# K transposed by VectorE in 32x32 word blocks, scores with a block-diagonal q

## The chip, the cores and the metric

The kernel runs on one core of one Trainium2 chip. The time is device time in microseconds (us) of one execution; the number that counts is the median of several executions without a profile. The engines of a core work side by side and meet at semaphores: TensorE (PE) multiplies matrices, with the loading of its weights shown as a row of its own (PEld); VectorE (DVE) and ScalarE (ACT) work on elements; GpSimd (POOL) only clears buffers here; SyncE (SP) issues the loads. Sixteen DMA engines move data between HBM and the on-chip memory SBUF. PE writes its results into PSUM, a second on-chip memory of eight banks.

## The reference

It is one decode step: attention of one token over a long cache, mixed with a small MLP by a gate. In bfloat16, cut to what matters:

```
x: 1 x 448;  k_cache, v_cache: 8 heads x 65536 rows x 256;  wq: 448 x 4096;  wo: 4096 x 448
q = (x @ wq)                         # 16 query heads of 256, two for each head of K and V
scores = q . k * 256 ** -0.5         # 16 x 65536
o = softmax(scores) @ v              # 16 x 256
a = o @ wo                           # 1 x 448
b = the MLP of layernorm(x)          # 1 x 448, 1792 hidden units, weights of length 1792
g = sigmoid(sum(x * gate_w))
out = g * a + (1 - g) * b
```

K and V are 268 MB each, so 537 MB are read to make 448 numbers.

## The kernel before, in words

**Blocks.** The cache is worked on in 32 blocks (`NBLK`), four for each K/V head. A block has 16384 rows of one head; each of the 128 SBUF partitions gets 128 consecutive rows. So a block has 8.4 MB of K, loaded as two halves into the tiles `kn0` and `kn1` (`load_k`, L109), and 8.4 MB of V, loaded into the one tile `vt` (`load_v`, L115). The loads are issued on SP's queue in a fixed order: V of block n, then both halves of K of block n+1, then V of block n+1. Each waits until its tile has been read: a half of K for the transposes of the block before, V for the products of the block before. `wo` (3.7 MB) follows after the K of block 1. In the last block V goes into the freed `kn` tiles in eight pieces that get smaller (`load_v_last`, L124). V of the block before the last comes in two parts, 48 rows for each partition before the last K and 80 behind it.

**Scores (`score_block`, L349).** To multiply q with K, the 256 elements of a row must lie across partitions. The kernel reads two bfloat16 neighbours as one 32-bit word and has PE transpose 128x128 words at a time (L326); four of them fill a PSUM bank `tps`, and DVE copies the bank into `kT` (L331). There are two `kT` tiles and four `tps` banks. A `kT` tile holds 16 rows of each partition (index i, 0 to 7), so a block has 8 such steps and 32 quarters. With `kT` in place, `scores` (L340) multiplies: for each of the two elements of a word (c), four matmuls of 32 columns of `qpad` against 512 columns, each in its own quarter of the PE array. All 8 steps add into one bank `sc_ps`: partition 32a + 2i + r holds the scores of step i, quarter a and query head r. `qpad` has zeros everywhere but in the two columns of its step.

**Softmax and products.** `softmax` (L400) takes the maximum over the bank, exchanges it between partitions by small matmuls, lets ACT take the exponential into `p_sb`, and has DVE transpose that into `pT` in 32x32 blocks (L432). `products` multiplies `pT` with V: 64 matmuls (L368), four of which run side by side. `accumulate` (L442, L447) adds the result, rescaled, to `acc`.

**End.** In the last block the pieces of V go through `columns` (L393), where the block of V is the weight, as they land. Then one DVE instruction makes `oT` (L579), four matmuls with `wo` (L584) add into one PSUM row `f_ps` that already holds the rest of the result, DVE copies its first half (L588), ACT its second (L589), and the row is stored (L590).

**Order.** The helper `seq` ties every instruction to the one before it on its engine, so each engine works in the order in which the program names its instructions. Between the quarters of a block small pieces of other work are hooked in: `gate_sum` and `mixer_tail` in block 0, `gate_column` in block 1, and in the last block `result_base` and a part of the products of the block before.

Of the kernel before, what the change touches and what calls it, by code (L numbers as in the profile page):

```python
# [8 lines left out]
FP32 = mybir.dt.float32  # L9
BF16 = mybir.dt.bfloat16  # L10
# [4 lines left out]
HQ = 16  # L15
HKV = 8
DH = 256
REP = HQ // HKV
# [3 lines left out]
KP = VP // 2  # L22
NJ = 16
NI = VP // NJ


@with_exitstack
def kernel(
# [15 lines left out]
    nc = tc.nc  # L44

    D = A_x.shape[-1]
# [4 lines left out]
    NB = SK // BLK  # L51
    NBLK = HKV * NB
# [36 lines left out]
    hd_ps = psum.tile([128, 512], FP32, name="hd_ps")  # L89

# [84 lines left out]
    qpad = const.tile([128, 2, HKV, NI, 32], BF16)  # L175
    seq(nc.gpsimd.memset(qpad[:], 0.0))


    xm = const.tile([128, 3], BF16)
# [62 lines left out]
    for h in range(HQ):  # L242
        half, hh = divmod(h, HQ // 2)
        for c in range(2):
# [13 lines left out]
                start=False,  # L258
                stop=True,
            ))  # L260
    seq(nc.vector.tensor_copy(
        out=qpad[:, :, :, 0, 0:REP],
        in_=q_ps.rearrange("p (c g r) -> p c g r", c=2, r=REP),
    ))
# [52 lines left out]
    base = const.tile([1, D], FP32)  # L317
    res = const.tile([1, D], BF16)
    gcol = const.tile([128, 1], FP32)
    state = {"t": 0}  # L320

    def transposes(i, quarter):
        tp = tps[state["t"] % 4]
        state["t"] += 1
        for jj in range(4):
            seq(nc.tensor.transpose(  # L326
                tp[:, jj * 128:(jj + 1) * 128],
                k_tiles[i // 4][:, i % 4 * NJ + quarter * 4 + jj, :].bitcast(FP32),
                ident_f[:, :],
            ))  # L330
        seq(nc.vector.tensor_copy(  # L331
            out=kT_tiles[i % 2][:, quarter * 4:(quarter + 1) * 4, :, :].rearrange(
                "p j n c -> p (j n c)"
            ),
            in_=tp[:, :].bitcast(BF16),
        ))

    def scores(g, i, c):
        for a in range(4):
            seq(nc.tensor.matmul(  # L340
                sc_ps[32 * a:32 * (a + 1), :],
                lhsT=qpad[:, c, g, i, :],
                rhs=kT_tiles[i % 2][:, :, 32 * a:32 * (a + 1), c],
                start=(i == 0 and c == 0),
                stop=(i == NI - 1 and c == 1),
                tile_position=(0, 32 * a),
            ))

    def score_block(n, hooks={}):  # L349
        due = []  # L350
        for t, (i, quarter) in enumerate((i, q) for i in range(NI) for q in range(4)):
            transposes(i, quarter)
            if due and due[0][0] <= t:
                scores(n // NB, *due.pop(0)[1])
            if quarter == 3:
                due.append((t + 2, (i, 0)))
                due.append((t + 3, (i, 1)))
            if t in hooks:
                hooks[t]()
        while due:  # L360
            scores(n // NB, *due.pop(0)[1])

    def pv(n, ip, jjs=range(NJ), tile=None, dst=pv_ps, last_ip=NI // 2 - 1):
        pT = pT_tiles[n % 2]
# [35 lines left out]
    def softmax(n, fill=None):  # L400
        b = n % NB
        fill = fill or [lambda: None] * 3
        nb, nb_old = nb_tiles[n % 2], nb_tiles[(n + 1) % 2]
        al, pT = al_tiles[n % 2], pT_tiles[n % 2]
        seq(nc.vector.tensor_reduce(out=rmax[:], in_=sc_ps[:, :], op=ALU.max, axis=AXIS.X))  # L405
        fill[0]()
        seq(nc.tensor.transpose(sm_ps[0:1, 0:128], rmax[:, 0:1], ident_f[:, :]))  # L407
        fill[1]()
        seq(nc.vector.tensor_reduce(  # L409
            out=(mrun if b == 0 else mnew)[:],  # L410
            in_=sm_ps[0:1, 0:128].rearrange("o (a i r) -> o r a i", a=4, r=REP)[:, :, :, 0:NI],
            op=ALU.max, axis=AXIS.XY,
        ))
# [10 lines left out]
        seq(nc.scalar.activation(  # L424
            out=p_sb[:, :], in_=sc_ps[:, :], func=ACT.Exp, scale=scale,
            bias=nb[:, 0:1], accum_out=den[:, 0:1],
        ))
# [4 lines left out]
        seq(nc.vector.transpose(out=pT[:, :], in_=p_sb[:, :]))  # L432
        if b > 0:
            seq(nc.vector.scalar_tensor_tensor(  # L434
                out=lsum[:], in0=lsum[:], scalar=al[:, 0:1], in1=den[:], op0=ALU.mult, op1=ALU.add
            ))
        else:
            seq(nc.vector.tensor_copy(out=lsum[:], in_=den[:]))
# [68 lines left out]
            op0=ALU.mult, op1=ALU.add,  # L507
        ))

    pv_last = sc_ps[:].rearrange("p (e d) -> p e d", e=2)  # L510
    o_last = hd_ps[:, 464:464 + 2 * REP].rearrange("p (c r) -> p c r", c=2)

    for n in range(NBLK):
        if n == 0:
            score_block(n, {8: gate_sum, 20: mixer_tail})
        elif n < L:
            score_block(n, {5: gate_column} if n == 1 else {})
        else:
            score_block(n, {4: result_base, 8: lambda: pv(L - 1, 0), 14: lambda: pv_one(L - 1, 2)})
        if n < L - 1:  # L520
            load_v(n)
            load_k(n + 1, 0)
            load_k(n + 1, 1)
            if n == 0:
                seq(nc.sync.dma_start(
                    out=wo_sb[:], in_=A_wo.rearrange("(h p c) n -> p h c n", p=128, c=2)
                ))
        elif n == L - 1:
            load_v(n, 0, 48)
            load_k(L, 0)  # L530
            load_k(L, 1)
            load_v(n, 48, VP)
        else:
            load_v_last(L)
        if n < L:
            softmax(n)
        else:
            def rest_base():
                seq(nc.tensor.matmul(
                    f_ps, lhsT=ident_f[0:1, 0:1], rhs=base[0:1, :], start=True, stop=False  # L540
                ))
                pv(L - 1, 2, range(4, NJ))

            f_ps = tps[0][0:1, 0:D]
# [36 lines left out]
    ))  # L581
    for c in range(2):
        for r in range(REP):
            seq(nc.tensor.matmul(  # L584
                f_ps, lhsT=oT[:, c, r:r + 1], rhs=wo_sb[:, HQ - REP + r, c, :],
                start=False, stop=(r == REP - 1 and c == 1),
            ))
    seq(nc.vector.tensor_copy(out=res[:, 0:D // 2], in_=f_ps[:, 0:D // 2]))  # L588
    seq(nc.scalar.copy(out=res[:, D // 2:], in_=f_ps[:, D // 2:]))  # L589
    seq(nc.sync.dma_start(out=out[0, 0].rearrange("(o n) -> o n", o=1), in_=res[:]))  # L590


# [28 lines left out]
```

## Time and profile before

| | us |
|---|---|
| median of 3 executions (1280.61 to 1280.92) | 1280.71 |
| the profiled execution | 1283.39 |
| its span, first to last instruction | 1281.6 |
| PE busy, 8663 matmuls | 986.4 |
| PE weight loads, 8663 | 642.5 |
| DVE busy, 1359 instructions | 755.2 |
| ACT busy | 43.1 |

The mean granted clock of PE is 0.853 of its full speed. The DMA engines moved 545.5 MB, 426 GB/s over the span. Busy time of PE is that of pipelined matmuls, so it overlaps itself. In rows of a group, "x1024 | 647.9, 684" means 1024 instructions, 647.9 us busy, 684 ns for one. In a timeline a row begins with its start and its length in us.

The trace also keeps one record for each packet that a DMA engine moved: its queue, its start, its bytes and how long it took. A half of K is 128 packets of 32 KB, eight for each DMA engine; a block of V is 128 packets of 64 KB, again eight for each.

### The profile page before, as it was taken

Reading aid. Unit: us, or ns where it says so; the run is one execution under the profiler, and the core shown is the slowest. Engines: PE = TensorE matmul, PEld = TensorE weight load, DVE = VectorE, ACT = ScalarE, POOL = GpSimd, SP = SyncE. Lnnn points to the kernel's source line nnn. Section 1 sums busy time; section 2 is a strip of 40 time slices with the busy share of each in tenths; the row PEclk is TensorE's granted clock in tenths of the full one; section 3 lists DMA queues with packets and bytes.
Section 4 is the critical chain, followed back from the end, with each engine's and each line's share of the span. In section 5 each row is a group of like instructions: output and inputs, shape, how many; then the busy total and the mean of one; then the engine's idle time right before and its main releaser. Section 6 shows DMA issues by size and latency. Waiting matters only on the chain.

```text
span 1281.6 us, 19942 instructions
## 1 busy us (share of the span) xinstructions
PE 986.4 (77%) x8663; PEld 642.5 (50%) x8663; DVE 755.2 (59%) x1359; ACT 43.1 (3%) x108; POOL 4.2 (0%) x7
## 2 busy tenths in 40 slices
PE   5777777797778777777876687866779777888796
PEld 4455444554545555445544455544456444555464
DVE  5464556665556655566654566644676545675483
ACT  4000000000000000000000000000000000000000
POOL 1000000000000000000000000000000000000000
PEclk9887878887888978789888889887898878898797
DMA  9999999999999999999999999999999999999896
GB/s 408 425 435 430 434 423 433 432 435 432 443 418 435 436 440 427 429 428 438 435 430 434 432 427 431 441 436 426 426 435 434 440 420 433 427 422 438 379 408 292
DMA packets 18000, 545.51 MB, mean 426 GB/s; under 512 B 2165, under 2 KB 4216, under 8 KB 4728
## 3 DMA queue, kind: packets, MB, share of 16 engines
q1 hardware_dynamic: 17474, 544.22, 98.7%
q8 instruction: 68, 1.11, 0.3%
q14 instruction: 20, 0.16, 0.0%
q10 hardware_dynamic: 438, 0.01, 0.0%
HBM read 544.22 MB, written 0.00 MB: 425 GB/s over the span
## 4 chain that ended last, share of the span: by engine, by line
DMA 69%; PE 29%; DVE 1%; issue 0%; SPq 0%; ACT 0%
DMA kn<-in_A_k_cache_dram 66%; PE tps L326 24%; PE sc_ps L340 5%; DMA vt<-in_A_v_cache_dram 2%; DMA kn<-in_A_v_cache_dram 2%; DVE kT L331 1%; PE tps L584 0%; DMA xr<-in_A_x_dram 0%; DVE z L279 0%; DVE zt L278 0%; DVE res L588 0%; PE hd_ps L393 0%; PE sm_ps L499 0%; ACT res L589 0%; SPq L109 0%
## 5 line engine op out<-in xcount | busy, mean ns | idle before, releaser
L331 DVE COPY kT<-tps 128x1024 bf16<-128x1024 bf16 x1024 | 647.9, 684 | 178.0 <-PE tps L326 176.9
L326 PE MATMUL tps<-ident_f,kn 128*128 128x128 f32 x4096 | 608.0, 298 | 99.3 <-DMA kn<-in_A_k_cache_dram 99.3
L326 PEld LDWEIGHTS tps<-ident_f,kn 128*128 128x128 f32 x4096 | 490.6, 152 | 220.3 <-DMA kn<-in_A_k_cache_dram 113.4
L368 PE MATMUL pv_ps<-vt,pT 128*4 128x512 bf16 x1968 | 175.1, 533 | 90.0 <-DMA vt<-in_A_v_cache_dram 84.3
L340 PE MATMUL sc_ps<-kT,qpad 128*32 128x512 bf16 x2048 | 201.8, 394 | 27.3 <-DVE kT L331 27.0
L368 PEld LDWEIGHTS <-pT 128*4 128x4 bf16 x2000 | 59.2, 109 | 197.9 <-issue 137.6
L442 DVE SCALAR_TENSOR_TENSOR acc<-acc,al,pv_ps 128x512 f32<-128x512 f32 x23 | 17.2, 747 | 157.7 <-PE pv_ps L368 157.7
L340 PEld LDWEIGHTS <-qpad 128*32 128x32 bf16 x2048 | 53.1, 93 | 110.3 <-issue 101.7
L424 ACT ACTIVATE p_sb<-sc_ps,nb 128x512 bf16<-128x512 f32 x32 | 22.0, 687 | 1204.3 <-DVE nb L420 1204.3
L447 DVE COPY acc<-pv_ps 128x512 f32<-128x512 f32 x8 | 5.5, 691 | 59.4 <-PE pv_ps L368 59.4
L432 DVE STREAM_TRANSPOSE pT<-p_sb 128x512 bf16<-128x512 bf16 x32 | 22.8, 711 | 28.9 <-ACT p_sb L424 28.9
L405 DVE TENSOR_REDUCE rmax<-sc_ps 128x1 f32<-128x512 f32 x32 | 22.1, 692 | 23.0 <-PE sc_ps L340 23.0
L407 PE MATMUL sm_ps<-ident_f,rmax 128*1 128x128 f32 x32 | 8.9, 279 | 24.9 <-DVE rmax L405 24.9
L416 PE MATMUL sm_ps<-mrun,ones_f 1*128 1x2 f32 x64 | 15.2, 304 | 13.8 <-DVE mrun L415 11.4
L407 PEld LDWEIGHTS sm_ps<-ident_f,rmax 128*1 128x1 f32 x32 | 2.5, 79 | 40.6 <-DVE rmax L405 40.6
L416 PEld LDWEIGHTS sm_ps<-mrun,ones_f 1*128 1x128 f32 x64 | 12.4, 241 | 20.3 <-DVE mrun L415 16.3
L420 DVE CUSTOM_DVE_ANT_0 junk<-sm_ps,nval 128x2 f32<-128x2 f32 x32 | 5.1, 159 | 18.1 <-PE sm_ps L416 18.1
L450 PE MATMUL hd_ps<-lsum,same 128*128 128x1 f32 x14 | 4.0, 358 | 13.8 <-DVE lsum L434 13.8
L450 PEld LDWEIGHTS hd_ps<-lsum,same 128*128 128x128 f32 x14 | 3.5, 307 | 14.5 <-DVE lsum L434 14.5
L409 DVE TENSOR_REDUCE mnew<-sm_ps 1x2 f32<-1x64 f32 x24 | 5.1, 212 | 9.0 <-PE sm_ps L407 9.0
L236 ACT ACTIVATE wo_sb<-h_bc,b1f,w1f 128x448 bf16<-128x448 f32 x14 | 9.2, 752 | 5.6 <-DVE h_bc L231 5.6
L464 PE MATMUL hd_ps<-esc,acc 128*128 128x2 f32 x28 | 4.4, 263 | 6.0 <-DVE acc L442 6.0
(100 smaller groups left out, 120.7 us busy)
## 6 DMA issues: line engine op xcount, KB each, us to landing
kn<-in_A_k_cache_dram SPq DMA_DIRECT2D x63, 4096.0 KB, 26.7
vt<-in_A_v_cache_dram SPq DMA_DIRECT2D x1, 5120.0 KB, 27.4
kn<-in_A_k_cache_dram SPq DMA_DIRECT2D x2, 2048.0 KB, 12.0
kn<-in_A_v_cache_dram SPq DMA_DIRECT2D x2, 2048.0 KB, 20.7
wo_sb<-in_A_wo_dram SPq DMA_DIRECT2D x1, 3584.0 KB
vt<-in_A_wq_dram SPq DMA_DIRECT2D x1, 3072.0 KB, 10.1
vt<-in_A_v_cache_dram SPq DMA_DIRECT2D x1, 3072.0 KB
kn<-in_A_v_cache_dram SPq DMA_DIRECT2D x3, 1024.0 KB, 20.4
```

Source lines behind the costliest of these rows:

```text
L236: seq(nc.scalar.activation(out=gel[:, b, :], in_=h_bc[:], func=ACT.Gelu_apprx_tanh, scale=w1f[:, b:b + 1], bias=b1f[:, b:b + 1],))
L326: seq(nc.tensor.transpose(tp[:, jj * 128:(jj + 1) * 128], k_tiles[i // 4][:, i % 4 * NJ + quarter * 4 + jj, :].bitcast(FP32), ident_f[:, :],))
L331: seq(nc.vector.tensor_copy(out=kT_tiles[i % 2][:, quarter * 4:(quarter + 1) * 4, :, :].rearrange("p j n c -> p (j n c)"), in_=tp[:, :].bi ...
L340: seq(nc.tensor.matmul(sc_ps[32 * a:32 * (a + 1), :], lhsT=qpad[:, c, g, i, :], rhs=kT_tiles[i % 2][:, :, 32 * a:32 * (a + 1), c], start=( ...
L368: seq(nc.tensor.matmul(dst[32 * grp:32 * grp + 2 * REP, :, :], lhsT=pT[:, 32 * jj + 2 * REP * ip:32 * jj + 2 * REP * (ip + 1)], rhs=pairs( ...
L405: seq(nc.vector.tensor_reduce(out=rmax[:], in_=sc_ps[:, :], op=ALU.max, axis=AXIS.X))
L407: seq(nc.tensor.transpose(sm_ps[0:1, 0:128], rmax[:, 0:1], ident_f[:, :]))
L416: seq(nc.tensor.matmul(sm_ps[:, 128:128 + REP], lhsT=ones_f[0:1, :], rhs=mrun[0:1, :], start=True, stop=True))
L424: seq(nc.scalar.activation(out=p_sb[:, :], in_=sc_ps[:, :], func=ACT.Exp, scale=scale, bias=nb[:, 0:1], accum_out=den[:, 0:1],))
L432: seq(nc.vector.transpose(out=pT[:, :], in_=p_sb[:, :]))
L442: seq(nc.vector.scalar_tensor_tensor(out=acc[:], in0=acc[:], scalar=al_tiles[n % 2][:, 0:1], in1=src[:, :, :], op0=ALU.mult, op1=ALU.add,))
L450: seq(nc.tensor.matmul(hd_ps[:, 460:461], lhsT=same[:].rearrange("p a r -> p (a r)"), rhs=lsum[:, 0:1], start=True, stop=True,))
```

## The change

The words of K are no longer transposed by PE. DVE transposes them itself, straight from `kn` into `kT`: one instruction for each step i, over 2048 words of each partition, in blocks of 32x32 words. The PSUM banks `tps` and DVE's copies out of them are gone. A 32x32 block stays within its 32 partitions, so `kT` now holds something else: partition 32a + k has word 32w + k of a row that belongs to partition 32a and its neighbours, and the words of a row are spread over four values of w (`NW`).

So q is laid out in another way. `sel` and four matmuls copy the 32 words of each w into all four quarters (`qq`), and `place_q` writes them as a block-diagonal matrix into `qz`, once for each head (in the second block of the head before; two tiles in turn). The scores of a step are eight matmuls (four w, two elements of a word) of 128 columns of `qz` against 512 columns; the step's place in the result is set by where in `qz` the 128 columns begin. `sc_ps` becomes two banks in turn. The last V block gets a bank of its own (`pv_last`).

At the end the result row is split in two halves of 224 in two PSUM banks, on partitions 0 and 32, each with its own matmuls; DVE copies one and ACT the other.

```diff
-    kT_tiles = [kvpool.tile([128, NJ, 128, 2], BF16, name=f"kT{i}") for i in range(2)]
+    kT_tiles = [kvpool.tile([128, NJ, NW, 32, 2], BF16, name=f"kT{i}") for i in range(2)]
...
-    tps = [psum.tile([128, 512], FP32, name=f"tps{i}") for i in range(4)]
-    sc_ps = psum.tile([128, 512], FP32, name="sc_ps")
+    sc_tiles = [psum.tile([128, 512], FP32, name=f"sc{i}") for i in range(2)]
...
+    pv_last = psum.tile([128, 2, DH], FP32, name="pv_last")
+    MC = D // 2
+    f_tiles = [psum.tile([64, MC], FP32, name=f"f{i}") for i in range(2)]
+    f_rows = [f_tiles[k][32 * k:32 * k + 1, :] for k in range(2)]
...
-    for i in range(1, NI):
-        seq(nc.vector.tensor_copy(
-            out=qpad[:, :, :, i, i * REP:(i + 1) * REP], in_=qpad[:, :, :, 0, 0:REP]
-        ))
+    for w in range(NW):
+        seq(nc.tensor.matmul(
+            qq_ps[:, w * 2 * HQ:(w + 1) * 2 * HQ],
+            lhsT=sel[:, w, :, :].rearrange("p a k -> p (a k)"), rhs=qb[:],
+            start=True, stop=True,
+        ))
...
+    def place_q(g):
+        for a in range(NQ):
+            quad = slice(32 * a, 32 * (a + 1))
+            seq(nc.vector.tensor_copy(
+                out=qz_tiles[g % 2][quad, :, 2 * NI + 32 * a:2 * NI + 32 * a + REP],
+                in_=qq[quad, :, g * REP:(g + 1) * REP],
+            ))
...
-        for jj in range(4):
-            seq(nc.tensor.transpose(
-                tp[:, jj * 128:(jj + 1) * 128],
-                k_tiles[i // 4][:, i % 4 * NJ + quarter * 4 + jj, :].bitcast(FP32),
-                ident_f[:, :],
-            ))
-        seq(nc.vector.tensor_copy(
-            out=kT_tiles[i % 2][:, quarter * 4:(quarter + 1) * 4, :, :].rearrange(
-                "p j n c -> p (j n c)"
-            ),
-            in_=tp[:, :].bitcast(BF16),
-        ))
+    def transposes(i):
+        seq(nc.vector.transpose(
+            out=kT_tiles[i % 2][:].rearrange("p j w k c -> p (j w k c)").bitcast(FP32),
+            in_=k_tiles[i // 4][:, i % 4 * NJ:(i % 4 + 1) * NJ, :].rearrange("p j d -> p (j d)").bitcast(FP32),
+        ))
...
+    def scores(n, i):
+        for w in range(NW):
+            for c in range(2):
+                seq(nc.tensor.matmul(
+                    sc_tiles[n % 2][:, :],
+                    lhsT=qz_tiles[n // NB % 2][:, 2 * w + c, 2 * (NI - i):2 * (NI - i) + 128],
+                    rhs=kT_tiles[i % 2][:, :, w, :, c],
+                    start=(i == 0 and w == 0 and c == 0),
+                    stop=(i == NI - 1 and w == NW - 1 and c == 1),
+                ))
...
+        for i in range(NI):
+            transposes(i)
+            scores(n, i)
+            if i in hooks:
+                hooks[i]()
+        if n % NB == 1 and n < NBLK - NB:
+            place_q(n // NB + 1)
...
-            score_block(n, {4: result_base, 8: lambda: pv(L - 1, 0), 14: lambda: pv_one(L - 1, 2)})
+            score_block(n, {1: result_base, 2: lambda: pv(L - 1, 0), 3: lambda: pv_one(L - 1, 2)})
...
-            seq(nc.tensor.matmul(
-                f_ps, lhsT=oT[:, c, r:r + 1], rhs=wo_sb[:, HQ - REP + r, c, :],
-                start=False, stop=(r == REP - 1 and c == 1),
-            ))
-    seq(nc.vector.tensor_copy(out=res[:, 0:D // 2], in_=f_ps[:, 0:D // 2]))
-    seq(nc.scalar.copy(out=res[:, D // 2:], in_=f_ps[:, D // 2:]))
+            for k in range(2):
+                seq(nc.tensor.matmul(
+                    f_rows[k], lhsT=oT[:, c, r:r + 1],
+                    rhs=wo_sb[:, HQ - REP + r, c, k * MC:(k + 1) * MC],
+                    start=False, stop=(r == REP - 1 and c == 1),
+                    tile_position=(0, 32 * k),
+                ))
+    seq(nc.vector.tensor_copy(out=res[:, 0:MC], in_=f_rows[0]))
+    seq(nc.scalar.copy(out=res[:, MC:], in_=f_rows[1]))
```

More of the change, by code (lines that the diff above doesn't have):

```diff
@@ L24 @@
 NI = VP // NJ
+NQ = 4
+NW = DH // 2 // 32
+QW = 128 + 2 * NI
 @with_exitstack
@@ L174 @@
     seq(nc.vector.memset(pv_ps[:], 0.0))
-    qpad = const.tile([128, 2, HKV, NI, 32], BF16)
-    seq(nc.gpsimd.memset(qpad[:], 0.0))
+    seq(nc.vector.memset(pv_last[:], 0.0))
+    qz_tiles = [const.tile([128, 2 * NW, QW], BF16, name=f"qz{i}") for i in range(2)]
+    for i in range(2):
+        seq(nc.gpsimd.memset(qz_tiles[i][:], 0.0))
+    sel = const.tile([128, NW, NQ, 32], BF16)
+    seq(nc.vector.tensor_copy(
+        out=sel[:],
+        in_=ident[:].rearrange("p (w k) -> p w k", w=NW).unsqueeze(2).to_broadcast([128, NW, NQ, 32]),
+    ))
     xm = const.tile([128, 3], BF16)
@@ L260 @@
             ))
-    seq(nc.vector.tensor_copy(
-        out=qpad[:, :, :, 0, 0:REP],
-        in_=q_ps.rearrange("p (c g r) -> p c g r", c=2, r=REP),
-    ))
-    for i in range(1, NI):
-        seq(nc.vector.tensor_copy(
-            out=qpad[:, :, :, i, i * REP:(i + 1) * REP], in_=qpad[:, :, :, 0, 0:REP]
-        ))
+    qb = work.tile([128, 2 * HQ], BF16)
+    seq(nc.vector.tensor_copy(out=qb[:], in_=q_ps))
+    qq_ps = sm_ps[:, 0:NW * 2 * HQ]
+    for w in range(NW):
[3 more added lines that the diff above has]
+            start=True, stop=True,
+        ))
+    qq = const.tile([128, 2 * NW, HQ], BF16)
+    seq(nc.vector.tensor_copy(out=qq[:], in_=qq_ps.rearrange("p (w h) -> p w h", h=HQ)))
+    def place_q(g):
+        for a in range(NQ):
+            quad = slice(32 * a, 32 * (a + 1))
+            seq(nc.vector.tensor_copy(
+                out=qz_tiles[g % 2][quad, :, 2 * NI + 32 * a:2 * NI + 32 * a + REP],
+                in_=qq[quad, :, g * REP:(g + 1) * REP],
+            ))
+    place_q(0)
     zt = work.tile([1, D], FP32)
@@ L319 @@
     gcol = const.tile([128, 1], FP32)
[L320 to L324, printed above, removed]
-        for jj in range(4):
-            seq(nc.tensor.transpose(
-                tp[:, jj * 128:(jj + 1) * 128],
-                k_tiles[i // 4][:, i % 4 * NJ + quarter * 4 + jj, :].bitcast(FP32),
-                ident_f[:, :],
-            ))
-        seq(nc.vector.tensor_copy(
-            out=kT_tiles[i % 2][:, quarter * 4:(quarter + 1) * 4, :, :].rearrange(
-                "p j n c -> p (j n c)"
-            ),
-            in_=tp[:, :].bitcast(BF16),
-        ))
@@ L338, in scores @@
[L338 to L346, printed above, removed]
-            ))
-    def score_block(n, hooks={}):
[L350 to L361, printed above, removed]
+    def transposes(i):
+        seq(nc.vector.transpose(
+            out=kT_tiles[i % 2][:].rearrange("p j w k c -> p (j w k c)").bitcast(FP32),
+            in_=k_tiles[i // 4][:, i % 4 * NJ:(i % 4 + 1) * NJ, :].rearrange("p j d -> p (j d)").bitcast(FP32),
+        ))
@@ L402, in softmax @@
         fill = fill or [lambda: None] * 3
+        sc_ps = sc_tiles[n % 2]
         nb, nb_old = nb_tiles[n % 2], nb_tiles[(n + 1) % 2]
@@ L508, in result_base @@
         ))
-    pv_last = sc_ps[:].rearrange("p (e d) -> p e d", e=2)
     o_last = hd_ps[:, 464:464 + 2 * REP].rearrange("p (c r) -> p c r", c=2)
@@ L514 @@
         if n == 0:
-            score_block(n, {8: gate_sum, 20: mixer_tail})
+            score_block(n, {2: gate_sum, 5: mixer_tail})
         elif n < L:
-            score_block(n, {5: gate_column} if n == 1 else {})
+            score_block(n, {1: gate_column} if n == 1 else {})
         else:
-            score_block(n, {4: result_base, 8: lambda: pv(L - 1, 0), 14: lambda: pv_one(L - 1, 2)})
+            score_block(n, {1: result_base, 2: lambda: pv(L - 1, 0), 3: lambda: pv_one(L - 1, 2)})
         if n < L - 1:
@@ L538, in rest_base @@
             def rest_base():
-                seq(nc.tensor.matmul(
-                    f_ps, lhsT=ident_f[0:1, 0:1], rhs=base[0:1, :], start=True, stop=False
-                ))
+                for k in range(2):
+                    seq(nc.tensor.matmul(
+                        f_rows[k], lhsT=ident_f[0:1, 0:1], rhs=base[0:1, k * MC:(k + 1) * MC],
+                        start=True, stop=False, tile_position=(0, 32 * k),
+                    ))
                 pv(L - 1, 2, range(4, NJ))
-            f_ps = tps[0][0:1, 0:D]
             softmax(n, [lambda: pv_one(L - 1, 3), lambda: pv(L - 1, 2, range(4)), rest_base])
@@ L583 @@
         for r in range(REP):
-            seq(nc.tensor.matmul(
-                f_ps, lhsT=oT[:, c, r:r + 1], rhs=wo_sb[:, HQ - REP + r, c, :],
-                start=False, stop=(r == REP - 1 and c == 1),
-            ))
-    seq(nc.vector.tensor_copy(out=res[:, 0:D // 2], in_=f_ps[:, 0:D // 2]))
-    seq(nc.scalar.copy(out=res[:, D // 2:], in_=f_ps[:, D // 2:]))
+            for k in range(2):
+                seq(nc.tensor.matmul(
+                    f_rows[k], lhsT=oT[:, c, r:r + 1],
[5 more added lines that the diff above has]
+    seq(nc.scalar.copy(out=res[:, MC:], in_=f_rows[1]))
     seq(nc.sync.dma_start(out=out[0, 0].rearrange("(o n) -> o n", o=1), in_=res[:]))
```

## The prediction

> **What bounds the kernel now.** I read the page's first three parts, then the chain that ended last, then the timeline of one block, of the block before the last and of the end.
>
> ```profile
> PE 986.4 (77%) x8663; PEld 642.5 (50%) x8663; DVE 755.2 (59%) x1359; ACT 43.1 (3%) x108; POOL 4.2 (0%) x7
> ...
> DMA  9999999999999999999999999999999999999896
> ...
> q1 hardware_dynamic: 17474, 544.22, 98.7%
> q8 instruction: 68, 1.11, 0.3%
> ```
>
> The DMA engines are busy everywhere but in the last slices. The loads (q1) take 98.7% of all engine time; a second customer, the fetching of instructions (q8), takes 68 packets of 1.11 MB / 68 = 16.3 KB, 256 instructions of 64 bytes each. PE and DVE have room.
>
> The chain of waits, from its list in order of time, confirms it: each block begins when its K lands.
>
> ```profile
> 109.65 5.38 PE tps L326 x24
> ...
> 1204.96 5.38 PE tps L326 x24
> ```
>
> These are blocks 2 and 30: 1095.31 us for 28 blocks, 39.12 us each. What would the engines need? By the packet records 64 KB take 2.418 us and 32 KB 1.213 us, whatever PE and DVE do meanwhile; 8 packets of V and 16 of K are 38.75 us, and 38.69 is the spacing at which the foremost engines begin one V after another from 117 to 1007 us. So 39.12 - 38.69 = 0.43 us a block are lost on the engines that come last. The records name the loss: a fetch takes 0.88 to 0.97 us on one engine, and the data packet behind it 0.46 to 0.55 us longer. The lengths of the fetches recur in a cycle of eight, so eight engines take them in turn; the others run ahead, and the spread between first and last engine of a V load grows from 2.0 us (block 1) to 11.2 (block 25). A load has landed when its last engine is done, so the engines with fetches set the time. From 109.65 to 1204.96 us there are 58 fetches: 0.43 x 28 / 58 = 0.206 us of the whole kernel for each, near (0.92 + 0.5) / 8 = 0.18.
>
> Is anything else late? In the timeline of block 15, V's issue follows the products by 0.05 us, and stands some 10 us ahead of its turn, since 8.4 MB of K (19.4 us) are still queued when V before it lands at 607.96.
>
> ```profile
> 607.96 6.45 PE L368 MATMUL pv_ps<-vt,pT 128*4 128x512 bf16 x64 [3.05 <-DMA vt<-in_A_v_cache_dram]
> ...
> 614.46 0.33 SPq L115 DMA_DIRECT2D vt<-in_A_v_cache_dram  x1
> ```
>
> **The change part by part.**
>
> *Instructions.* 4096 transposes with 4096 weight loads go (8192), and 1024 copies become 256 instructions (768 fewer); score matmuls stay 64 a block; start and end add some ten. 8960 x 64 bytes / 16 KB = 35 fetches fewer, 33 left. At 0.206 us: **-7.2 us**. Bounds: by the packets 0.178 x 35 = 6.2, and one step of a last engine (1.4 us) up or down by where the cycle of eight stops; nothing, if the fetches were not what the last engines lose by.
>
> The Trainium skill speaks against this term: "Runtime: NRT & Kernel Launch", Instruction fetch mechanics, says that crossing a 16 KiB block costs a tail bump that is mostly hidden. By it the term is nothing and the sum 1279.1. The records of this trace disagree, with 0.9 us on an engine that has no gap; the rule looks at the engine that waits for code, not at the data behind it.
>
> *DVE.* The trace has no transpose of 32-bit words. The nearest row:
>
> ```profile
> L331 DVE COPY kT<-tps 128x1024 bf16<-128x1024 bf16 x1024 | 647.9, 684 | 178.0 <-PE tps L326 176.9
> ...
> L340 PE MATMUL sc_ps<-kT,qpad 128*32 128x512 bf16 x2048 | 201.8, 394 | 27.3 <-DVE kT L331 27.0
> ...
> L432 DVE STREAM_TRANSPOSE pT<-p_sb 128x512 bf16<-128x512 bf16 x32 | 22.8, 711 | 28.9 <-ACT p_sb L424 28.9
> L405 DVE TENSOR_REDUCE rmax<-sc_ps 128x1 f32<-128x512 f32 x32 | 22.1, 692 | 23.0 <-PE sc_ps L340 23.0
> ...
> L409 DVE TENSOR_REDUCE mnew<-sm_ps 1x2 f32<-1x64 f32 x24 | 5.1, 212 | 9.0 <-PE sm_ps L407 9.0
> ```
>
> 512 elements transposed take 711 ns. The two reductions give the slope: (692 - 212) / 448 = 1.07 ns an element, so some 0.16 us are fixed. 2048 words are 2048 x 1.07 + 0.16 = 2.35 us if a word costs what an element costs, and 4.5 us if it costs two. I take 2.35: the reductions of 32-bit elements run at the same pace as the transpose of 16-bit ones. A block is 18.8 us of DVE against 32 x 0.684 = 21.9 before.
>
> What hides it: DVE's own cycle in a block is 8 transposes, the last scores (2 us), the softmax (reduction to `pT`: 603.03 to 606.73, 3.7 us), the products (6.45) and `accumulate` (0.75): 8T + 12.9. It stays under 39 us up to T = 3.2 us. New waits: a transpose waits for the scores two steps back (`kT`), and behind it on DVE stand only the next transposes and the softmax; SP's loads of K wait for the transposes in place of PE's. With T = 2.35 a half of K is free after 9.4 us, 11.5 before (617.62 to 629.17). At zero, then, under cover of 39 us of loads.
>
> *PE.* A score matmul of 128 columns has the array to itself. In the timeline 4 side by side take 0.40 us and 8 take 0.62, so a pass of 512 columns is 0.22 us at full clock; 64 products in 6.45 us make 0.40 for a pass at half clock. Eight passes are 1.8 us, 3.3 at half clock; under DVE's 2.35 or a little over. Nothing on the path.
>
> *The block before the last.* Its V comes as 3 MB, so the next K has less cover:
>
> ```profile
> 1217.93 11.16 SPq L109 DMA_DIRECT2D kn<-in_A_k_cache_dram  x2
> ```
>
> K of block 31 is issued 12.97 us after K landed at 1204.96. By the packet records seven engines then stand idle, the others end V at 1219.0 to 1219.6, and the first packets take 1.3 to 2.1 us for 1.21; at 1229.2 to 1230.0 a third of a us is lost again, since the second half is issued when the first is through. With transposes by DVE the issue comes after 9.4 to 11.7 us (the later figure with PE cold in the first two steps): **-0.5** (0 to -0.9).
>
> *The end.*
>
> ```profile
> 1276.40 0.37 PE L393 MATMUL hd_ps<-pT,kn 128*128 128x2 bf16 x8 [0.27 <-DMA kn<-in_A_v_cache_dram]
> ...
> 1277.02 1.65 PE L584 MATMUL tps<-wo_sb,oT 128*1 128x448 bf16 x4 [0.25 <-DVE oT L579]
> ...
> 1278.71 0.38 DVE L588 CAST res<-tps 1x224 bf16<-1x224 f32 x1 [1.75 <-PE tps L584]
> 1279.13 0.34 ACT L589 CAST res<-tps 1x224 bf16<-1x224 f32 x1 [18.20 <-DVE res L588]
> ```
>
> ACT waits for DVE's copy. In the changed kernel it waits for PE alone: -0.4. Four matmuls of 448 columns (0.37 each at half clock, 0.16 to begin) become four pairs of 224 in different quarters: 0.91 us if a pair runs side by side, as L340's and L368's fours do, 1.65 if not. -0.7 (0 to -0.7). Together **-1.1**.
>
> *The start.* `sel`, `qq`, `place_q` and a second clearing of PSUM add some 2 us before the first transpose at 18 us. The next load to need it, K of block 1, has its turn behind V of block 0, at 49 us: nothing; a cost would need 20 us more. `place_q` (4 small copies, each about the 0.18 us of a small DVE instruction) runs where DVE idles.
>
> **Sum.** -7.2 - 0.5 - 1.1 = -8.8 us. The profiled execution took 1283.39 (span 1281.6 and 1.8 around it), 2.7 more than the median; it would fall to 1274.6 and the median from 1280.71 to **1271.9**. If those 2.7 us go with the number of instructions, the median gains 1.2 less.
>
> **The rivals.**
>
> *The fetches cost nothing on the whole* (the other engines' lead is slack, and the 0.43 us a block has another cause): only the two small terms stay, 1279.1. For it: 0.3% of engine time is little. Against: the spread grows with the fetches. Chance 0.13.
>
> *A word costs DVE two elements' time.* T = 4.5 us, past the point of 3.2. Then DVE sets the block: 8 x 4.5 + 12.9 = 48.9 us, 31 x 9.9 = 307 us more, 1588 us. For it: no row shows a 32-bit transpose. Against: L405. Chance 0.06.
>
> *PE stays at half clock.* It would wait for DVE between steps, and after idle stretches the clock is low:
>
> ```profile
> 605.00:610.00 5.00, 2.04 (x20) 0.74 (x24) 0.93 (x4) 0.96 (x3) 0.00 (x0) 0.69 0.97 419
> 610.00:615.00 5.00, 4.41 (x48) 1.35 (x40) 0.53 (x1) 0.00 (x0) 0.00 (x0) 0.63 0.97 416
> ```
>
> At half clock for good, PE's cycle is 8 x 3.3 to 3.44, the first transpose 2.35, softmax 3.7, products 6.45, `accumulate` 0.75: 40.2 us, 1.2 above the loads, 37 us in all: 1309. It decides from a mean pass of some 3.2 us a step. Against: at half clock PE has no gap (3.4 against 2.35), and from 625 us on, a few us into steady work, the clock is 1.00. "TensorE: Matmul & The Clock Gate" of the Trainium skill, A second HAM failure mode, tells of clocks that swing when PE idles briefly between groups; swinging gives about 2.9 us a step, still covered. Chance 0.03.
>
> **How the numbers follow.** The forecast has 0.78. Its own range: -7.2 with a step of 1.4 at the most one way and 1.2 (profile) with 1.0 (packet price) the other, and the bounds of the small terms, is 1270.3 to 1275.7. The range is drawn on to the first rival, 1279.2, and leaves out the two slow ones and the rims. Faster by over 0.2% (below 1278.15; 0.2% is about what a measurement of this kernel tells from no change) is the forecast and a little of the first rival between, 0.79; within 0.2% the rest of that rival, 0.12; slower 0.09.
>
> **What would show it.** Right: some 33 fetch packets, K landing every 38.9 us, 256 DVE transposes of 2.3 to 2.4 us, ACT's and DVE's last copies starting together, no late issue of the last K. Wrong: transposes over 3.2 us with loads of K issued behind their turn; or half the fetches with landings still 39.1 us apart.

## The result, and the profile after

The changed kernel takes 1272.74 us (median of 6 executions, 1272.4 to 1272.92) against 1280.74 beside it: 8.0 us less, a ratio of 0.9937 (95% interval 0.9924 to 0.9949). The forecast was 1271.9.

First the page of the changed kernel: busy time, DMA engines, DMA queues, and the two groups that replace PE's transposes.

```profile
span 1270.5 us, 10379 instructions
...
PE 781.2 (61%) x4577; PEld 305.4 (24%) x4577; DVE 684.2 (54%) x619; ACT 43.1 (3%) x108; POOL 2.7 (0%) x8
...
q1 hardware_dynamic: 17474, 544.22, 99.3%
q8 instruction: 35, 0.57, 0.2%
...
q14 instruction: 10, 0.07, 0.0%
...
L356 PE MATMUL sc<-kT,qz 128*128 128x512 bf16 x2048 | 550.5, 419 | 248.8 <-DVE kT L348 248.5
L348 DVE STREAM_TRANSPOSE kT<-kn 128x2048 f32<-128x2048 f32 x256 | 571.4, 2284 | 129.8 <-DMA kn<-in_A_k_cache_dram 80.6
```

A transpose of 2048 words takes 2.28 us. The loads now take 99.3% of the DMA engines' time, 98.7% before. There are 35 packets of queue 8 in place of 68, and 10 of queue 14 in place of 20. Both pairs turned out to matter. On the page before, the second queue was this line:

```profile
q14 instruction: 20, 0.16, 0.0%
```

The chain of waits, at the start of blocks 2 and 30:

```profile
109.50 2.32 DVE kT L348
...
1196.82 2.32 DVE kT L348
```

1087.32 us for 28 blocks, 38.83 each, where it was 39.12: what the stream of loads gives comes evenly, block by block. The block before the last, on SP's queue, and the end:

```profile
1207.87 9.19 SPq L115 DMA_DIRECT2D kn<-in_A_k_cache_dram  x2
```

```profile
1266.28 0.37 PE L403 MATMUL hd_ps<-pT,kn 128*128 128x2 bf16 x8 [0.27 <-DMA kn<-in_A_v_cache_dram]
...
1266.90 0.91 PE L596 MATMUL f<-wo_sb,oT 128*1 128x224 bf16 x8 [0.26 <-DVE oT L590]
1267.85 0.38 DVE L602 CAST res<-f 1x224 bf16<-1x224 f32 x1 [1.00 <-PE f L596]
1267.88 0.34 ACT L603 CAST res<-f 1x224 bf16<-1x224 f32 x1 [18.11 <-PE f L596]
```

The last K is issued 11.05 us after the K before it landed, 12.97 before. The eight small matmuls take 0.91 us, and the copies run side by side.

The two profiled executions are further apart than the medians: 1283.39 to 1272.5, because the profiled execution before lies 2.7 us above its own median and the one after does not. So the 8.0 us by which the 28 blocks got shorter (1095.31 less 1087.32) are not the 8.0 us between the medians. The accounts below go by medians.

### The profile page after: what moved, and what is told of

Read it like the earlier page. It is cut to its first block, busy times and chain, and to the rows that moved or that the text cites. A ratio compares the mean times of both kernels' runs of the same rounds, so it can differ in the third digit from the quotient of the medians.

```text
span 1270.5 us, 10379 instructions
## 1 busy us (share of the span) xinstructions
PE 781.2 (61%) x4577; PEld 305.4 (24%) x4577; DVE 684.2 (54%) x619; ACT 43.1 (3%) x108; POOL 2.7 (0%) x8
## 3 DMA queue, kind: packets, MB, share of 16 engines
q1 hardware_dynamic: 17474, 544.22, 99.3%
## 4 chain that ended last, share of the span: by engine, by line
DMA 71%; PE 13%; DVE 12%; issue 3%; ACT 0%; ACTq 0%; SPq 0%; DVEq 0%
DMA kn<-in_A_k_cache_dram 66%; PE sc L356 12%; DVE kT L348 12%; DMA vt<-in_A_v_cache_dram 2%; DMA kn<-in_A_v_cache_dram 2%; DMA w1b<-in_B_w_dram 1%; PE pv_ps L378 0%; PE hd_ps L315 0%; PE f L596 0%; ACT p_sb L435 0%; DVE pT L443 0%; DVE rmax L416 0%; DVE y_sb L319 0%; DVE rest L325 0%; ACTq L135 0%
## 5 line engine op out<-in xcount | busy, mean ns | idle before, releaser
L356 PE MATMUL sc<-kT,qz 128*128 128x512 bf16 x2048 | 550.5, 419 | 248.8 <-DVE kT L348 248.5
L348 DVE STREAM_TRANSPOSE kT<-kn 128x2048 f32<-128x2048 f32 x256 | 571.4, 2284 | 129.8 <-DMA kn<-in_A_k_cache_dram 80.6
L356 PEld LDWEIGHTS <-qz 128*128 128x128 bf16 x2048 | 210.4, 104 | 587.3 <-issue 228.2
L435 ACT ACTIVATE p_sb<-sc,nb 128x512 bf16<-128x512 f32 x32 | 22.0, 687 | 1193.0 <-DVE nb L431 1193.0
L416 DVE TENSOR_REDUCE rmax<-sc 128x1 f32<-128x512 f32 x32 | 22.1, 692 | 60.4 <-PE sc L356 60.4
L427 PE MATMUL sm_ps<-mrun,ones_f 1*128 1x2 f32 x64 | 12.1, 256 | 13.8 <-DVE mrun L426 11.3
L427 PEld LDWEIGHTS sm_ps<-mrun,ones_f 1*128 1x128 f32 x64 | 9.3, 182 | 20.0 <-DVE mrun L426 16.0
L486 PE MATMUL hd_ps<-wo_sb,oT 128*1 128x448 bf16 x28 | 7.3, 351 | 0.0
L440 ACT ACTIVATE al<-nb,nb 128x1 f32<-128x1 f32 x24 | 6.8, 282 | 0.0
L260 PE MATMUL hd_ps<-xm,vt 128*128 128x1 bf16 x96 | 3.7, 165 | 4.6 <-DMA vt<-in_A_wq_dram 4.6
```

The source lines that it names most:

```text
L348: seq(nc.vector.transpose(out=kT_tiles[i % 2][:].rearrange("p j w k c -> p (j w k c)").bitcast(FP32), in_=k_tiles[i // 4][:, i % 4 * NJ:(i ...
L356: seq(nc.tensor.matmul(sc_tiles[n % 2][:, :], lhsT=qz_tiles[n // NB % 2][:, 2 * w + c, 2 * (NI - i):2 * (NI - i) + 128], rhs=kT_tiles[i % ...
L427: seq(nc.tensor.matmul(sm_ps[:, 128:128 + REP], lhsT=ones_f[0:1, :], rhs=mrun[0:1, :], start=True, stop=True))
L435: seq(nc.scalar.activation(out=p_sb[:, :], in_=sc_ps[:, :], func=ACT.Exp, scale=scale, bias=nb[:, 0:1], accum_out=den[:, 0:1],))
L440: seq(nc.scalar.activation(out=al[:], in_=nb_old[:], func=ACT.Exp, scale=-1.0, bias=nb[:, 0:1]))
L486: seq(nc.tensor.matmul(a_ps, lhsT=oT[:, c, r:r + 1], rhs=wo_sb[:, g * REP + r, c, :], start=(r == 0 and c == 0), stop=(r == REP - 1 and c ...
```

## The experiments

Two things were to be told apart: whether the gain is due to the fetching of instructions (the DMA packets of queues 8 and 14) at all, and which fetches. Rival 1 was that K is free earlier, rival 2 that PE no longer reads K. All medians stand against 1280.7 to 1281.2 us of the kernel before on the same chip; "the changed kernel" is the 1272.74 of the result. It was not run again beside the others, and the kernel before moved by 0.5 us between the groups of runs, so a difference of less than that says nothing.

### Idle instructions on PE

```diff
+    def pad(count):
+        for _ in range(count):
+            seq(nc.tensor.matmul(
+                sm_ps[:, 300:301], lhsT=ident[:], rhs=ident[:, 0:1], start=True, stop=True
+            ))
...
         if n < L - 1:
             if n % NB == NB - 1:
                 denominators()
+            pad(149)
             products(n)
```

> The changed kernel with 149 idle pairs (a weight load and a matmul of one column, into a column of PSUM that nobody reads) ahead of the products of each of the first 30 blocks: 8940 instructions more, 35 fetch packets, about what the change took away. They run where PE waits for V. Theory (the time goes with the fetch packets, 0.18 to 0.21 us of the whole kernel for each): 6.2 to 7.2 us more than the changed kernel's 1272.7, so 1278.9 to 1279.9, with some 71 fetch packets. Rival 1 (the gain is that DVE frees K earlier) and rival 2 (the gain is that PE no longer reads K): 1272.7, since neither is touched.

Measured: 1278.7 us (1278.26 to 1278.89), ratio to before 0.9982 (0.9973 to 0.9991): 6.0 us over the changed kernel, a little under the 6.2 to 7.2 expected. Page, DMA queues:

```profile
q8 instruction: 70, 1.15, 0.3%
...
q14 instruction: 9, 0.07, 0.0%
```

Instructions that do nothing, in a stretch in which PE mostly waits anyway, give back three quarters of the gain, where both rivals expected no change. The padding does not hold the loads up either: on the foremost DMA engine the V loads still begin 38.68 us apart up to 929 us. So fetches cost time here.

> The same with 298 pairs, 70 packets more. Theory: 12.4 to 14.4 us over 1272.7, 1285.1 to 1287.1, twice the step of 149 pairs. The pairs take some 9.5 us, 3.5 more than PE's idle stretch, so V is issued later, within its lead of 10 us. Rivals 1 and 2: 1272.7.

Measured: 1371.09 us (1357.15 to 1382.93), ratio 1.0666 (1.0619 to 1.0713). This is far beyond twice the step. The timeline of one block and the waits of SP and PE:

```profile
601.19 3.78 PE L525 MATMUL sm_ps<-ident 128*128 128x1 bf16 x143 [0.26 <-DVE nb L431]
...
608.37 3.55 PE L525 MATMUL sm_ps<-ident 128*128 128x1 bf16 x128 [3.40 <-issue]
...
615.39 0.86 PE L525 MATMUL sm_ps<-ident 128*128 128x1 bf16 x27 [3.47 <-issue]
616.18 5.93 PE L378 MATMUL pv_ps<-vt,pT 128*4 128x512 bf16 x64
622.16 0.33 SPq L121 DMA_DIRECT2D vt<-in_A_v_cache_dram  x1
```

```profile
SPq L121 <- PE pv_ps L378: 573.1, 30, 24.4
```

PE works off 128 pairs, 256 instructions, in 3.6 us and then stands still for 3.4 us with nothing to wait for that the profile shows, and then the same again. That is one fetch packet's worth of instructions each time. The products end late, and the load of V is issued late: SP waits for them up to 24.4 us. So this run says nothing on the price of a fetch; it is a new wait, and it is what made the forecast of this run wrong.

### Fewer instructions in the kernel before

```diff
-        for jj in range(4):
+        for jj in (0, 3):
             seq(nc.tensor.transpose(
```

(The four `tps` banks are cleared once at the start.)

> The kernel before with two of the four transposes of each PSUM bank left out (the scores of half the rows are those of stale words; DVE's copies, the scores and all loads are as before): 4096 instructions fewer, 16 fetch packets. Theory: 2.8 to 3.3 us under 1280.7, so 1277.4 to 1277.9, with 52 packets. Rival 1: 1280.7, since DVE's copies still set when K is free. Rival 2: half of the stream's gain, 3.5 us, so this run doesn't tell it from the theory; the idle pairs do.

Measured: 1281.09 us (1280.82 to 1281.52), ratio 1.0001 (0.9993 to 1.001). Nothing, against 2.8 to 3.3 us expected; the theory of the prediction misses here. Page, DMA queues:

```profile
q8 instruction: 52, 0.85, 0.2%
q14 instruction: 20, 0.16, 0.0%
```

The packets of queue 8 did go, 68 to 52. Those of queue 14 did not. The packet records show what was overlooked: each 8 KB packet of queue 14 also stops one DMA engine, 0.30 us for itself and 0.55 us on the data packet behind it, 0.855 together. The page counts the 20 that fall in the span (six more come ahead of it), and most of them are DVE's: the trace has 2183 records of DVE, 821 of which do nothing but wait for a semaphore, and at 64 bytes each that is 2183 / 128 = 17 packets, 15 of them in the span. In the changed kernel it is 822 records, 6.4 packets, five of them in the span. And the spread between first and last engine of a V load, in the kernel before and in this run alike, grows by 0.85 us every two blocks, the pace of queue 14, not by 1.4 us for every eight packets of queue 8. In the changed kernel it grows by 1.42 us for eight packets of queue 8. The prediction had read the growth as that of queue 8 in the kernel before.

The new theory: lost time adds up for each DMA engine by itself, and a load has landed when the slowest has. DVE's fetches all fall on one engine (15 in the span x 0.855 = 12.8 us), PE's on eight in turn (68 / 8 x 1.42 = 12.1 us). The larger of the two sets the time, not the sum.

The records don't name the engines, but they can be followed: a busy engine starts each packet within 0.02 us of the end of the one before. Between 100 and 1190 us of the changed kernel this gives 16 chains. Five packets of queue 14, those at 246, 476, 673, 867 and 1095 us, lie on one chain without any packet of queue 8; the 29 packets of queue 8 lie on eight other chains, three or four on each. In the kernel before, the chains come too close to each other to be told apart to the end, but there too the first ten packets of DVE (125 to 795 us) lie on one. The next four runs show what follows for the time.

> The changed kernel with 32 idle clearings of one word by DVE in each of the first 30 blocks, where DVE waits for the products: 960 instructions, 7.5 packets of 8 KB on queue 14. New theory (each DMA engine's lost time adds up for itself, and a load lands with the slowest engine; a packet of queue 14 costs 0.30 of its own and 0.55 on the data behind it, always on one engine for DVE; a packet of queue 8 costs 1.42 on one of eight in turn): the engine of DVE's packets loses 13 to 14 x 0.855 = 11.1 to 12.0 us and becomes the slowest, past the 4.5 x 1.42 = 6.4 of the others, so 4.7 to 5.6 us over 1272.7: 1277.4 to 1278.3. Theory of the prediction (every fetched byte costs alike, spread over eight engines): 123 KB on queue 14 are worth 3.75 packets of 16 KB, 0.7 us: 1273.4. Rival (fetches cost nothing): 1272.7.

```diff
+    def pad(count):
+        for _ in range(count):
+            seq(nc.vector.memset(dsink[:], 0.0))
...
         if n < L - 1:
+            pad(32)
```

Measured: 1276.93 us (1276.82 to 1277.35), ratio 0.9968 (0.9956 to 0.9981): 4.2 us over the changed kernel. Page, queues and the padding:

```profile
q8 instruction: 35, 0.57, 0.2%
q14 instruction: 17, 0.14, 0.0%
```

```profile
L529 DVE MEMSET dsink<- 128x1 f32 x960 | 56.6, 59 | 61.1
```

960 instructions on DVE cost 4.2 us; 8940 on PE cost 6.0. For each instruction that is 6.5 times as much. The even price of the prediction gave 0.7 us. The new theory gave 4.7 to 5.6, so it is a little high; with the 13 packets of DVE that the records hold in the span it is the 4.7. One more thing could have cost the time: PE's products now wait for the padding.

```profile
L378 PE MATMUL pv_ps<-vt,pT 128*4 128x512 bf16 x1968 | 182.4, 550 | 162.2 <-DMA vt<-in_A_v_cache_dram 109.6 <-DVE dsink L529 52.6
```

But the loads don't come later for it. On the foremost engine the last whole V load begins at 1161.67 us, in the changed kernel at 1161.36; what grew is the spread, from 6.1 us to 11.0.

> The same 960 idle instructions, 32 a block, on ACT in place of DVE (small copies, after its softmax work). They too come through queue 14, 7.3 packets more. New theory: if ACT's packets are on an engine of their own, that engine stays below the others (8 x 0.855 = 6.8 against 6.4), 1272.7 to 1273.2; if they share the engine of DVE's packets, 1277.4 to 1278.3 as with DVE. Theory of the prediction: 1273.4. Rival: 1272.7.

The edit is the same with `nc.scalar.copy(out=dsink[:], in_=dummy[:])`. Measured: 1272.8 us (1272.67 to 1273.93), ratio 0.9937 (0.9924 to 0.9951). No change, with nearly as many packets:

```profile
q8 instruction: 35, 0.57, 0.2%
q14 instruction: 16, 0.13, 0.0%
```

So it is not the number of queue 14's packets but whose they are. Followed through the records of this run, seven packets (217 to 1072 us) lie on one chain and DVE's five (246 to 1091 us) on another, and the 29 of queue 8 again on eight others: ACT's code comes over an engine of its own, one that had room.

> The kernel before with DVE's copies over two PSUM banks at once: 512 copies in place of 1024, 920 instructions of DVE's stream fewer with their waits, 7 packets of queue 14 fewer; PE's 68 packets of queue 8 stay. New theory: DVE's engine falls from some 12.8 us of loss to 6.7, but the eight engines of queue 8 keep theirs, 8.5 x 1.42 = 12.1, so the gain is 0 to 1.0 us: 1279.7 to 1280.7. Theory of the prediction: 7 packets of 8 KB, 0.6 us: 1280.1.

```diff
-    tps = [psum.tile([128, 512], FP32, name=f"tps{i}") for i in range(4)]
+    tps = [psum.tile([128, 1024], FP32, name=f"tps{i}") for i in range(2)]
...
-        seq(nc.vector.tensor_copy(
-            out=kT_tiles[i % 2][:, quarter * 4:(quarter + 1) * 4, :, :].rearrange(
-                "p j n c -> p (j n c)"
-            ),
-            in_=tp[:, :].bitcast(BF16),
-        ))
+        if odd:
+            seq(nc.vector.tensor_copy(
+                out=kT_tiles[i % 2][:, (quarter - 1) * 4:(quarter + 1) * 4, :, :].rearrange(
+                    "p j n c -> p (j n c)"
+                ),
+                in_=tp[:, :].bitcast(BF16),
+            ))
```

Measured: 1280.91 us (1279.6 to 1281.42), ratio 0.9995 (0.9986 to 1.0004). Page, DMA queues:

```profile
q8 instruction: 68, 1.11, 0.3%
...
q14 instruction: 13, 0.11, 0.0%
```

Less of DVE's code alone gives nothing that can be told from no change either. (Five of the eleven executions took 1279.6 to 1280.3 us, the others 1280.9 to 1281.4; the theory allows up to 1.0.)

> The kernel before with both: two of four transposes left out (the scores of half the rows are those of stale words) and copies over two banks. Packets: 52 of queue 8, 7 fewer of queue 14. New theory: now both kinds of engine are eased, the slowest loses 6.5 to 7 x 1.42 = 9.2 to 9.9 us in place of 12.8, so 2.9 to 3.6 us under 1280.7: 1277.1 to 1277.8, though leaving out the transposes alone gave nothing. Rivals 1 and 2 of the first runs: PE's reads alone gave nothing, so no gain here either, 1280.7.

Measured: 1276.75 us (1276.29 to 1278.82), ratio 0.9969 (0.9957 to 0.998): 4.2 us under the kernel before, with both:

```profile
q8 instruction: 52, 0.85, 0.2%
q14 instruction: 13, 0.11, 0.0%
```

This is more than the 2.9 to 3.6 us expected; the interval reaches from 2.6 to 5.5. Nothing from the one, nothing from the other, 4.2 us from both: by the medians that is a maximum of two, not a sum. (The intervals alone would just allow a sum: at most 0.9 and 1.8 us for the single edits, at least 2.6 for both.) It is also the second answer to rival 2, since PE's transposes of K were halved in the run with half the transposes without effect. The medians side by side, with the spread (last end less first start of the last whole V load, less its 19.34 us) from the packet records of the profiled execution:

```
kernel                        queue 8  queue 14  spread us   median us
before                             68        20      11.3    1280.74
half the transposes                52        20      12.0    1281.09
copies over two banks              68        13       8.7    1280.91
both                               52        13       6.2    1276.75
changed                            35        10       6.1    1272.74
changed, 32 on DVE                 35        17      11.0    1276.93
changed, 32 on ACT                 35        16       6.1    1272.8
changed, 149 pairs on PE           70         9       8.7    1278.7
```

The spread is not the loss itself: late in a run an engine that leads can be held up because its next load isn't issued yet, which shrinks the spread and costs nothing.

### The terms at the end

> The changed kernel with the end of before: one PSUM row of 448, four matmuls, ACT's copy behind DVE's. Prediction's term for the end: 1.1 us more than 1272.7 (0.7 for the matmuls side by side, 0.4 for the copies), 1273.8. Rival (the end is hidden behind the store): 1272.7.

```diff
-            for k in range(2):
-                seq(nc.tensor.matmul(
-                    f_rows[k], lhsT=oT[:, c, r:r + 1],
-                    rhs=wo_sb[:, HQ - REP + r, c, k * MC:(k + 1) * MC],
-                    start=False, stop=(r == REP - 1 and c == 1),
-                    tile_position=(0, 32 * k),
-                ))
-    seq(nc.vector.tensor_copy(out=res[:, 0:MC], in_=f_rows[0]))
-    seq(nc.scalar.copy(out=res[:, MC:], in_=f_rows[1]))
+            seq(nc.tensor.matmul(
+                f_ps, lhsT=oT[:, c, r:r + 1], rhs=wo_sb[:, HQ - REP + r, c, :],
+                start=False, stop=(r == REP - 1 and c == 1),
+            ))
+    seq(nc.vector.tensor_copy(out=res[:, 0:MC], in_=f_ps[:, 0:MC]))
+    seq(nc.scalar.copy(out=res[:, MC:], in_=f_ps[:, MC:]))
```

Measured: 1273.81 us (1273.45 to 1275.31), ratio 0.9945 (0.9933 to 0.9958): 1.07 over the changed kernel. The interval of the ratio is wider than that, so the 1.07 rests on the timeline as well. In the changed kernel the store is issued at 1268.30, 2.02 us after the last matmuls with V begin. Here, in the timeline of the same stretch:

```profile
1266.39 0.37 PE L403 MATMUL hd_ps<-pT,kn 128*128 128x2 bf16 x8 [0.27 <-DMA kn<-in_A_v_cache_dram]
...
1269.48 0.32 SPq L599 DMA_DIRECT2D out_dram<-res  x1
```

3.09 us: 1.07 us longer.

> The kernel before with V of the block before the last in two parts of 64 rows, in place of 48 and 80: the last K gets 2.4 us more cover and is issued before the engines run out. Prediction's term for the late issue: 0.5 us under 1280.7 (0 to 0.9), 1280.2. Rival (only engines that lead stood idle, and the slowest lost nothing): 1280.7.

```diff
-            load_v(n, 0, 48)
+            load_v(n, 0, 64)
...
-            load_v(n, 48, VP)
+            load_v(n, 64, VP)
```

Measured: 1280.51 us (1280.36 to 1282.1), ratio 0.9995 (0.9986 to 1.0004). Inconclusive: 0.2 to 0.7 us under the kernel before, depending on which of its medians is taken, and the interval holds no change.

> The same edit in the changed kernel, as a candidate: the last K is issued 11.1 us after the K before it landed, earlier than before, and by the packet records a third of the engines waited 1 us. 0 to 0.4 us under 1272.7.

Measured: 1272.52 us (1272.28 to 1273.69), ratio 0.9933 (0.9921 to 0.9946). This is not to be told from the changed kernel.

### The cover over DVE

> The changed kernel with three of the eight transposes of a block (steps 1, 3, 5) done twice: 11 in a block. Prediction: DVE's cycle is 11 x 2.21 + 12.9 = 37.2 us, still under the loads' 38.8, so the transposes cost nothing: 1272.7; only before the last block, where a half of K is then free after 13.3 us, may the loads wait 1 to 2 us: up to 1274.5. Rival 1 (the gain is that DVE frees K earlier): a half of K is free some 4 us later than in the changed kernel and later than before, so most of the gain is lost, 1279 or more.

```diff
     def transposes(i):
-        seq(nc.vector.transpose(
+      for _ in range(2 if i in (1, 3, 5) else 1):
+        seq(nc.vector.transpose(
```

Measured: 1274.75 us (1273.35 to 1277.01), ratio 0.9951 (0.9937 to 0.9964). Three more transposes in each block, 96 in all and 219 us of DVE's time, cost 2.0 us, 0.2 us more than the upper bound expected, and the executions spread widely. The traces show where, though the profiled execution is the slowest of the four: the last whole V load ends only 0.1 us later than in the changed kernel's trace, and the rest of the loss comes behind it. In the block before the last a half of K lands at 1198.10 and the last K is issued at

```profile
1211.71 11.44 SPq L115 DMA_DIRECT2D kn<-in_A_k_cache_dram  x2
```

13.6 us later, where it was 11.05 in the changed kernel. Rival 1 falls with it: K was free later in every block, and six of the eight us stayed (4.6 to 8.1 by the interval).

> The same with every transpose done twice, 16 in a block, as if a word cost two elements' time. Prediction: DVE's cycle is 16 x 2.21 + 12.9 = 48.3 us, 9.4 over the loads, so DVE sets the time: 30 x 9.4 = 282 us more, about 1555. If the cover were larger than the prediction has it, less than 1400.

The same edit for all eight steps. Measured: 1612.39 us (1610.79 to 1613.98), ratio 1.2584 (1.2561 to 1.2607). The group of the transposes, and SP's waits:

```profile
L349 DVE STREAM_TRANSPOSE kT<-kn 128x2048 f32<-128x2048 f32 x512 | 1157.1, 2292 | 8.8
```

```profile
SPq L115 <- DVE kT L349: 1148.8, 62, 24.3
SPq L121 <- PE pv_ps L379: 335.1, 30, 12.4
```

DVE has no idle time left ahead of its transposes (8.8 us) and SP waits for it. The cycle of a block, by the V loads' first packets, is 49.5 us, and 16 x 2.29 + 12.9 = 49.5. The expectation of 1555 was 57 us short: it took 2.21 us for a transpose, the step from one to the next in the changed kernel, where one takes 2.29 here, and it counted 30 blocks. At 49.5 us these make some 320 of the 340 us; the others lie in the last blocks.

## Why the prediction was right, point by point

**The bound.** Right. Loads take 99.3% of the engine time of the changed kernel, blocks begin when K lands, 38.8 us apart (38.9 forecast).

**The fetches, -7.2 us.** The direction and most of the size were right, the attribution was not, and that the size came so close is in part luck. The step that failed is "0.206 us of the whole kernel for each" of queue 8's packets, on the ground that eight engines take them in turn and "the engines with fetches set the time". It left out queue 14, whose 20 packets were on the page. In the kernel before, by the runs, the slowest engine is the one with DVE's code; 16 fewer packets on queue 8 gave nothing. The change lowers both at once: DVE's engine from 15 x 0.855 = 12.8 us to 5 x 0.855 = 4.3, the eight others from 12.1 to 36 / 8 x 1.42 = 6.4 (the records hold one packet of queue 8 more than the page counts). From the larger to the larger that is 12.8 - 6.4 = 6.4 us. It is an estimate from the mean of 4.5 packets an engine: with four on the slowest the gain is 7.1, with five 5.7. The price of 0.206 was measured on the slowest engine, DVE's, and divided by the packets of the others. So the term was some 0.8 us too large, and the same price was wrong where an edit touched only one of the two engines' code: it gave 2.8 to 3.3 us for half the transposes, which gave none, and 0.7 us for the padding on DVE, which cost 4.2.

**The rule weighed against this term.** The Trainium skill, in "Runtime: NRT & Kernel Launch", Instruction fetch mechanics, holds that the crossing of a 16 KiB block is mostly hidden. For PE's own work the runs agree until PE runs through its code quickly (149 pairs: one stop of some 3 us in a block, ahead of the products); for the loads they don't: 35 packets of queue 8 more cost 6.0 us.

**DVE, at nothing under cover.** Right: 2.28 us for a transpose where 2.35 was taken from the reductions' slope, so a word costs what an element costs. The point of decision was right too: 11 transposes fit under the loads in all blocks but the one before the last, 16 don't. The new waits are there (PE for `kT` 248.5 us in all) and cost nothing.

**PE, at nothing.** Right. Eight passes take 1.90 us at full clock, 3.6 in the first steps of a block at half clock. In block 15 the granted clock is 0.50 from 615 to 621 us and 1.00 from there on, so the rival in which it stays low did not come.

**The block before the last, -0.5 us.** The mechanism shows in the traces (12.97 us to 11.05), its size isn't settled: giving the kernel before more cover gave 0.2 to 0.7 us with an interval that holds nothing.

**The end, -1.1 us.** Right, 1.07, with both parts as costed: the matmuls take 0.91 us in place of 1.65, and the two copies together 0.38 in place of 0.76.

**The sum.** 6.4 + 0.5 + 1.1 = 8.0, the measured 8.0. That they meet to the tenth is chance: the 0.5 is the forecast's, not a measurement, and the 6.4 may be 5.7 to 7.1. The measured time lies 0.8 us over the forecast, by this account in the first term, and inside the range. (The rims of the prediction's own range are a little off: 1.4 and 0.4 under 1271.9 are 1270.1, and 1.2, 1.0, 0.5 and 0.7 over it are 1275.3. Nothing hangs on that.) Of the rivals none came; "the fetches cost nothing on the whole" is excluded by the idle instructions.

## What to carry to other kernels

Here the loads fill the DMA engines from end to end, and the instructions themselves are traffic. In such a kernel, read the instruction queues on the page, and ask which engine each stands in the way of, since a load lands with its slowest engine and only the largest loss counts. Then count instructions per engine, those that only wait included, and expect nothing from thinning one engine's code while another's sets the time. Work could be moved from PE to DVE under such loads at no cost as long as DVE's cycle in a block stayed below the load's; where a block has less cover, as the one before the last does, it cost 2 us.

## What the runs showed that was not expected

- A 16 KB fetch of PE's code costs its DMA engine 1.42 us of a stream of 64 KB and 32 KB packets (0.88 to 0.97 itself, 0.46 to 0.55 on the packet behind), an 8 KB fetch of DVE's 0.855, where the bytes alone would be 0.61 and 0.30 at the pace of 32 KB in 1.213 us.
- 960 idle instructions on DVE cost 4.2 us, the same number on ACT nothing, and 8940 on PE 6.0.
- DVE's code comes over one DMA engine, ACT's over another, and PE's over eight more in turn, by the packet records of the changed kernel and of the run with padding on ACT.
- PE can run out of code: with 298 idle pairs it stops for 3.4 us after every 256 instructions. That the fetch stands behind data packets of 2.4 us on its DMA engine is the likely reason, but no run shows it.
